# Giving the first eight pairs of a fused attention and gated network due times of their own

## The chip, the core and the metric

The kernel runs on one core of a Trainium2 chip. Its time is the device time of one execution, in microseconds (us); less is better. The engines are TensorE (PE in the profile's rows: matmuls; PEld: its weight loads), VectorE (DVE), ScalarE (ACT), GpSimd (POOL) and SyncE (SP), whose queue issues most transfers (DMA).

## What is computed

Eight batches of eight heads (576 positions, 64 per head, float32) go through rotary attention, and the result of all heads of a batch through a gated network with a causal convolution of 5 taps as its gate.

```python
q_rot, k_rot = rotate(q), rotate(k)            # (8, 8, 576, 64)
scores = scale * np.matmul(q_rot, k_rot.transpose(0, 1, 3, 2))
scores = scores - np.max(scores, axis=-1, keepdims=True)
attn = np.exp(scores)
attn = attn / (np.sum(attn, axis=-1, keepdims=True) + 1e-09)
x = np.matmul(attn, v)                         # heads joined: (8, 576, 512)
...
for k in range(5):
    gate_pre += conv_w[k] * xp[:, k:k + S, :]  # xp: x with 4 zeros in front
gate = 1.0 / (1.0 + np.exp(-gate_pre))
val = x @ w_val
return gate * val @ w_out
```

## The kernel before

The unit of work is a pair of heads, 32 in all, four to a batch. For a pair p the program loads k and q (`loadk`, `loadq`, on SP's queue), rotates them (`mul0`, `mul1`, `add`), splits them into a high and a low part (`hi` on ScalarE, `lo`), and multiplies them on TensorE in five chunks of queries: `s0` to `s3` for the two heads side by side, `s4` for the last 64 queries of both together. Each chunk's rows get a maximum on VectorE (`max0` to `max8`, line 261) and an exponential on ScalarE (`exp0` to `exp8`, line 274); `exp8` writes the tile `pm`. The probabilities are then transposed: in pairs 0 to 4 and in the last one by TensorE (`t0` to `t7`, line 303) with copies out of PSUM (`c0` to `c7`, lines 190 and 192), in the others by VectorE (`x1`, `x3`, `x5`, `x7`, one for each chunk, line 289) with 16 transfers (`mv`). The value products follow (`pv4`, `pv0`, `pv1`, lines 359 to 377), the division by the row sums (`norm`), and the taps of the convolution (`tap0` on ScalarE, `tap1` to `tap4` on VectorE, line 429). `xhi`, `xlo` split the result. After the fourth pair of a batch its network is added (`f00` to `f07` the first product, `f10` to `f17` the second, `od` its evictions, line 463 the matmuls). The weights arrive in pieces and are decoded early, between the first pairs (`lval`, `dval`, `lout`, `dout`); `taps`, `dtap` load and decode the convolution's factors. `warm0` to `warm4` are matmuls without a result that fill TensorE's first stretch.

Nothing of this is written down in the order in which it runs. Each job is given to a planner with a due time and with what it reads and writes; the planner takes the ready job with the earliest due time, again and again, and that order is the order on each engine's queue. So a job stands where the largest due time among itself and the jobs that it waits for puts it. A job that needs a buffer which is not free is parked until one is. The score chunks keep their order through a token (`order`). GpSimd jobs wait for the last VectorE job ahead of them that is marked as using the shared port.

The due time is a base, which grows by `PERIOD` = 18.5 for each pair, plus an offset from the table `DUE`, looked up by the job's name. Pairs 0 to 4 use names with an `e` at the end (`s0e`), pair 0's loads and rotary steps names with `_0` and `_1` for the two parts of the sequence, and all later pairs share one set. The table `PICK` tells for most elementwise steps, copies and transfers which engine does them (V, A, G, SP).

```python
heap = [(jobs[i][0], i) for i in range(len(jobs)) if not left[i]]
...
i = heappop(heap)[1]
...
t = PERIOD * p
...
at(f"s{c}" + ph, t + 3.6 * c, "PE", 830, s_mm, p, c, r=r, w=w + " order", mode="r" if c < 4 else "f")
at(f"max{i}" + ph, t + 3.6 * c + 1 + 0.7 * h, "V", 670, s_max, p, i, r=f"ps_s/{p}.{i}", w=f"nm/{p}.{i}")
at(f"x{i}" + ph, tt, "V", 1270, turn, p, i // 2, cs, r=r + f" p/{p}.{i // 2}#0", w=f"big/T{p}#{i // 2}")
```

Here `tt` is `t + 3.6 * (i // 2) + 3.6 + 0.7 * (i % 2)`. Buffers that matter here: three tiles for scores in PSUM (`ps_s`, one for each head's chunk), two for everything else in PSUM (`ps_t`), three tiles `p` for probabilities.

Of the kernel before, what the change touches and what calls it, by code (L numbers as in the profile page):

```python
# [144 lines left out]
def attn_gated_ffn(ctx: ExitStack, tc: tile.TileContext, q2, k2, v2, tab, w_val, conv_w, w_out, out, collect=None):  # L145
# [4 lines left out]
    V, A, G, T, SP = nc.vector, nc.scalar, nc.gpsimd, nc.tensor, nc.sync  # L150
# [6 lines left out]
    plan = Plan()  # L157
# [353 lines left out]
    taps = []  # L511
# [41 lines left out]
        for t in mixq:  # L553
            V.memset(t.bitcast(F32), 0.0)

    def at(key, base, e, ns, fn, *args, pick=None, r="", w="", kb=0, mode=None, port=False):

        options = ns if pick else None
        if pick:
            e = PICK.get(pick, e)  # L560
            ns, port = options[e]
            args = [ENG[e] if a == "ENGINE" else a for a in args]
        plan.add(base + DUE.get(key, 0.0), e, fn, *args, r=r, w=w, port=port)
        if collect is not None:
            collect.append((key, base, pick, options, ns, kb * (3.6 if fn is move else 2.95), mode, port or e == "G"))

# [34 lines left out]
    PERIOD = 18.5  # L601
    for p in range(NP):
        t = PERIOD * p
        par = p % 2
        last = p == NP - 1
        ph = "e" if p < EARLY else ""
        cs = TURNED.get(p, (0, 1, 2, 3) if p >= EARLY and not last else ())
        xt = toks(f"x{par}#@", range(5))
        for n in ("k", "q"):
            cut = 288 if n == "k" else 256  # L610
# [105 lines left out]
        last = b == NB - 1  # L716
# [92 lines left out]
```

## Time and profile before

| what | value |
|---|---|
| median of 3 runs | 649.25 us (648.69 to 650.76) |
| the profiled execution | 645.8 us, of it 644.0 us from the first to the last instruction (the span) |
| TensorE busy | 612.9 us (95%) |
| VectorE busy | 569.8 us (88%) |
| ScalarE busy | 463.7 us (72%) |
| GpSimd busy | 404.6 us (63%) |
| moved by DMA | 134.43 MB |
| granted TensorE clock, mean | 0.997 of full speed |

Times in the rows below are counted from the start of the span. Busy shares are means over stages that differ: an early one in which weights are decoded and probabilities are transposed on TensorE, a long steady one, and an end without new pairs. An engine that is idle costs nothing unless the last engine to finish waits for it.

### The profile page before, as it was taken

To read this page: it belongs to the slowest core of one execution; us is meant where nothing else is said; L and a number is where in the kernel's file an instruction comes from. 1 tells how busy PE (TensorE), PEld (TensorE's weight loads), DVE (VectorE), ACT (ScalarE), POOL (GpSimd) and SP (SyncE) were. 2 spreads that over 40 slices of the span, in tenths; PEclk is the share of its full clock that TensorE was granted. 3 is DMA by queue.
4 is the path that set the end of the run, shared out by engine and by line. 5 is a ranking of instruction groups with operands and counts; after the bars stand their busy time and mean duration, and the time that the engine had idled before them with its cause. 6 is when DMAs were issued, how large, how long until landed. Compare 5 with 4: busy or idle time off the path is not lost.

```text
span 644.0 us, 15384 instructions
## 1 busy us (share of the span) xinstructions
PE 612.9 (95%) x5683; PEld 502.1 (78%) x5683; DVE 569.8 (88%) x820; ACT 463.7 (72%) x1161; POOL 404.6 (63%) x304
## 2 busy tenths in 40 slices
PE   8899998989999999999999999999899999999897
PEld 8666665778787887888788887887688878888797
DVE  5998899988999999999999999999999999995452
ACT  4989988767777777777777768776777778765421
POOL 4433457776778868796868868785878768730300
PEclk9999999989999999999999999999999999999999
DMA  6524532379999999989999899898999998864011
GB/s 234 196 69 167 178 114 75 111 202 251 267 259 241 260 263 258 276 236 259 242 261 258 236 266 251 251 251 233 245 267 257 249 274 249 214 168 127 29 49 54
DMA packets 51482, 134.43 MB, mean 209 GB/s; under 512 B 10928, under 2 KB 20944, under 8 KB 51408
## 3 DMA queue, kind: packets, MB, share of 16 engines
q1 hardware_dynamic: 50864, 132.86, 73.1%
q8 instruction: 45, 0.74, 0.5%
q10 hardware_dynamic: 544, 0.59, 0.3%
q14 instruction: 29, 0.24, 0.1%
HBM read 62.48 MB, written 9.59 MB: 112 GB/s over the span
## 4 chain that ended last, share of the span: by engine, by line
PE 73%; DVE 13%; DMA 4%; ACT 4%; POOL 2%; issue 2%; SPq 1%; DVEq 0%; POOLq 0%; ACTq 0%
PE ps_t L463 29%; PE ps_s L255 17%; PE ps_t L369 17%; DVE nm L261 5%; PE ps_t L359 3%; DVE g L429 3%; DVE big L289 2%; PE ps_t L374 2%; PE ps_t L330 2%; ACT p L274 2%; DMA big<-big 2%; PE ps_t L303 1%; POOL xl L416 1%; DMA rb<-rd 1%; PE ps_t L345 1%
## 5 line engine op out<-in xcount | busy, mean ns | idle before, releaser
L261 DVE TENSOR_REDUCE nm<-ps_s 128x1 f32<-128x576 f32 x288 | 203.3, 743 | 18.2 <-PE ps_s L255 18.1
L274 ACT ACTIVATE p<-ps_s,nm 128x576 f32<-128x576 f32 x256 | 187.6, 738 | 34.1 <-DVE nm L261 31.2
L255 PE MATMUL ps_s<-k,q 64*128 64x288 f32 x1536 | 144.1, 311 | 11.7 <-ACT p L274 9.6
L289 DVE STREAM_TRANSPOSE big<-p 128x1152 f32<-128x1152 f32 x104 | 140.6, 1360 | 0.0
L255 PEld LDWEIGHTS ps_s<-k,q 64*128 64x128 f32 x1536 | 110.5, 185 | 36.1 <-issue 15.5
L429 DVE SCALAR_TENSOR_TENSOR g<-x,cw,g 128x576 f32<-128x576 f32 (+1 forms) x132 | 117.3, 890 | 1.8 <-ACT g L426 1.5
L369 PE MATMUL ps_t<-big,v 128*64 128x256 f32 (+2 forms) x1024 | 118.4, 382 | 0.0
L212 POOL TENSOR_TENSOR iq<-iq,tab 128x576 f32<-128x576 f32 (+2 forms) x60 | 84.6, 1428 | 35.7 <-DMA iq<-in_q 25.7
L369 PEld LDWEIGHTS ps_t<-big,v 128*64 128x64 f32 x1024 | 70.1, 137 | 44.6 <-issue 13.9
L463 PE MATMUL ps_t<-xh,wval_hi 128*128 128x288 f32 x256 | 79.7, 311 | 0.4 <-DVE x L405 0.3
L463 PE MATMUL ps_t<-yh,wout_hi 128*128 128x288 f32 x256 | 79.4, 311 | 0.0
L216 POOL TENSOR_TENSOR ik<-ik 128x576 f32<-128x576 f32 (+1 forms) x28 | 50.5, 1804 | 45.9 <-DVE ik L212 44.0
L463 PE MATMUL ps_t<-yl,wout_hi 128*128 128x288 f32 x256 | 76.3, 298 | 1.8 <-POOL yl L476 1.8
L463 PE MATMUL ps_t<-xl,wval_hi 128*128 128x288 f32 x256 | 76.5, 299 | 0.5 <-POOL xl L416 0.5
L463 PE MATMUL ps_t<-xh,wval_lo 128*128 128x288 f32 x256 | 76.0, 297 | 0.0
L463 PE MATMUL ps_t<-yh,wout_lo 128*128 128x288 f32 x256 | 76.0, 297 | 0.0
L476 POOL TENSOR_TENSOR yl<-g,yh 128x288 fp32r<-128x288 f32 x56 | 46.8, 835 | 46.4 <-ACT yh L472 42.6
L227 POOL TENSOR_TENSOR k<-ik,k 128x576 fp32r<-128x576 f32 x31 | 49.7, 1603 | 35.3 <-ACT k L223 35.1
L416 POOL TENSOR_TENSOR xl<-x,xh 128x576 fp32r<-128x576 f32 x31 | 47.7, 1538 | 20.2 <-ACT xh L412 18.3
L463 PEld LDWEIGHTS ps_t<-xh,wval_hi 128*128 128x128 f32 x256 | 49.1, 192 | 4.3 <-issue 2.3
L274 ACT ACTIVATION_READ_ACCUMULATOR p<-ps_s,nm 128x1 f32 x256 | 50.7, 198 | 0.0
L463 PEld LDWEIGHTS ps_t<-yh,wout_hi 128*128 128x128 f32 x256 | 48.9, 191 | 2.2 <-PE ps_s L255 1.8
(95 smaller groups left out, 1081.8 us busy)
## 6 DMA issues: line engine op xcount, KB each, us to landing
big<-big SPq DMA_DIRECT2D x416, 144.0 KB
ik<-in_k SPq DMA_DIRECT2D x31, 576.0 KB
iq<-in_q SPq DMA_DIRECT2D x31, 576.0 KB
v<-in_v SPq DMA_DIRECT2D x32, 320.0 KB
rb<-rd SPq DMA_DIRECT2D x64, 144.0 KB
out_t<-oo SPq DMA_DIRECT2D x64, 144.0 KB
big<-in_w_val SPq DMA_DIRECT2D x4, 512.0 KB
big<-in_w_out SPq DMA_DIRECT2D x4, 512.0 KB
```

What stands on the lines that cost most here:

```text
L212: eng.tensor_tensor(out=t[:, i, a:b], in0=t[:, i, a:b], in1=tabs[:, i, a:b], op=ALU.mult)
L216: eng.tensor_tensor(out=t[:, 0], in0=t[:, 0], in1=t[:, 1], op=ALU.add)
L227: eng.tensor_tensor(out=t[:, 1], in0=state[p][n + "in"][:, 0, a:b], in1=t[:, 0].bitcast(F32), op=ALU.subtract)
L255: T.matmul(out=ps[:, half, 0:288], lhsT=st["q"][rows, x, c * 128:c * 128 + 128] if c < 4 else mixq[p % 2][:, x], rhs=st["k"][rows, y, k0:k ...
L261: V.tensor_reduce(out=st[f"nm{i}"], in_=st[f"s{i}"], axis=AX.XY, op=ALU.max, negate=True)
L274: A.activation(out=pd.rearrange("p (b x) -> p b x", b=2), in_=st[f"s{i}"], func=AF.Exp, bias=st[f"nm{i}"], scale=1.0, accum_out=sums[p % 2 ...
L289: V.transpose(out=t[:, :, cs.index(c)].rearrange("p b k i -> p k b i"), in_=st[f"p{c}"].rearrange("p h s -> p (h s)").rearrange("p (k b i) ...
L369: T.matmul(out=acc[HEAD[h], 0:n], lhsT=st["v"][:, j, h, :], rhs=st["pt"][:, :, c0:c1, 5 * place(p, 2 * c0 + h) + j].rearrange("p a c i -> ...
L416: eng.tensor_tensor(out=st["xl"][:, a:b], in0=xs[p % 2][:, 4 + a:4 + b], in1=st["xh"][:, a:b].bitcast(F32), op=ALU.subtract)
L429: V.scalar_tensor_tensor(out=g, in0=x_sb[:, a + k:b + k], scalar=w, in1=g, op0=ALU.mult, op1=ALU.add)
L463: T.matmul(out=acc[:, 0:n], lhsT=wt[w][:, kc, ds], rhs=mv, start=(kc == 0 and i == 0), stop=(kc == NCH - 1 and i == 2))
L476: eng.tensor_tensor(out=ffn[b, "l", dc, lo], in0=y, in1=ffn[b, "h", dc, lo].bitcast(F32), op=ALU.subtract)
```

## The change

Three lines of code change: the lookups of `DUE` and `PICK` try the name with `@` and the pair's number first, for pairs 0 to 7 (`OWN` = 8). A batch's network is added inside its fourth pair's turn, so batches 0 and 1 use the numbers 3 and 7. `DUE` grows from 267 to 811 entries; the old ones without a number keep their values where pairs from 8 on use them. `PICK` grows from 98 to 270; 36 of its new entries name another engine than the old table, and no old one changes. `TURNED` is empty, so the line with it gives the same as before. The tables are cut below to entries that the text speaks of, one to a line.

```diff
+OWN = 8
...
-DUE = {
...
-'dtap': 18.1213, 'max0e': 14.6821, 'max1e': 13.2885, 'tap2e': 19.0603, 'tap3e': 21.309,
-'pv4e': 18.8053, 'loadke': -59.771, 'loadqe': -41.1482, 'lval0': -12.7532,
-'s0': 9.932, 's3': 21.9753, 's4': 23.5471, 'max0': 16.779, 'max1': 14.6677, 'max8': -12.7968,
-'exp6': -0.0862, 'x5': 22.804, 'x7': 22.26,
...
+DUE = {
...
+'dtap': -69.8201, 'max0e@0': -61.4337, 'max1e@0': -56.4516, 's0e@0': -10.8488, 'tap2e@4': 34.8082, 'tap3e@4': 43.1084,
+'pv4e@0': 19.0091, 'pv4e@1': 18.2196, 'pv4e@2': 18.1959, 'pv4e@3': 21.281, 'pv4e@4': 19.3977,
+'loadke@1': 25.2513, 'loadqe@1': 20.8687, 'lval0': -21.5969,
+'s3@5': 15.9488, 's4@5': -6.7157, 'max8@5': -8.7262, 'exp6@5': 20.7505, 'x5@5': 21.4718, 'x7@5': -16.7783,
+'s0@6': -11.4168, 'max0@6': -39.7509, 'max1@6': -3.4868,
...
+PICK: from G to V
+  'kadd_1@0', 'qmul1_0@0', 'qlo_0@0', 'qadd_1@0' (parts of the sequence),
+  'xloe@0', 'qmul1e@1', 'kmul1e@4', 'klo@5', 'qmul0@5', 'qadd@5', 'qmul0@6', 'qmul1@6', 'kmul0@7', 'klo@7'
+PICK: from V to G
+  'qmul0e@2', 'kmul1@5', 'kmul1@6', 'kmul1@7'
+PICK: from A to V
+  'c1e@0', 'c1e@1', 'c2e@1', 'cme@1', 'c6e@2', 'c3e@3', 'cme@3', 'cm@6',
+  'ch1e@3', 'qmixede@4', 'chm@7', 'od1@7', 'od2@7'
+PICK: from V to A
+  'c4e@1', 'c0e@2', 'c4e@2', 'c4e@3', 'c0e@4'
...
+    phase = [0]
+
     def at(key, base, e, ns, fn, *args, pick=None, r="", w="", kb=0, mode=None, port=False):
...
-            e = PICK.get(pick, e)
+            e = PICK.get(f"{pick}@{phase[0]}", PICK.get(pick, e))
...
-        plan.add(base + DUE.get(key, 0.0), e, fn, *args, r=r, w=w, port=port)
+        plan.add(base + DUE.get(f"{key}@{phase[0]}", DUE.get(key, 0.0)), e, fn, *args, r=r, w=w, port=port)
...
         t = PERIOD * p
+        phase[0] = p if p < OWN else ""
...
-        cs = TURNED.get(p, (0, 1, 2, 3) if p >= EARLY and not last else ())
+        cs = TURNED.get(-1 if last else p, (0, 1, 2, 3) if p >= EARLY and not last else ())
```

## Rows read from the trace of the kernel before

**Rows 1.** Busy us by stage: PE, PEld, DVE, ACT, POOL; then clock, DMA, GB/s.

```profile
0.00:20.00 20.00, 16.52 (x129) 14.98 (x130) 13.08 (x26) 9.76 (x21) 8.36 (x14) 1.00 0.72 255
20.00:120.00 100.00, 91.06 (x795) 63.49 (x793) 94.00 (x146) 87.33 (x209) 48.86 (x33) 1.00 0.35 118
120.00:180.00 60.00, 56.16 (x497) 47.65 (x498) 54.06 (x75) 43.42 (x113) 44.42 (x35) 0.97 0.84 229
180.00:560.00 380.00, 370.70 (x3593) 306.32 (x3592) 360.45 (x496) 286.37 (x730) 290.92 (x214) 1.00 0.92 253
```

**Rows 2.** The chain that ended last: start, length, what.

```profile
217.74 3.60 PE ps_t L369 x32
...
410.30 3.60 PE ps_t L369 x32
```

**Rows 3.** TensorE's waits from 20 to 180 us: total, times, longest.

```profile
PE ps_s L255 <- ACT p L274: 4.7, 8, 1.1
PE ps_t L303 <- ACT big L190: 2.1, 3, 1.1
PE ps_s L255 <- ACT pm L274: 2.0, 1, 2.0
```

**Rows 4.** Timeline of TensorE near 130 us (start, length, what, idle before).

```profile
129.40 1.06 PE L255 MATMUL ps_s<-k,q 64*128 64x288 f32 x12
132.43 0.40 PE L255 MATMUL ps_s<-k,q 64*128 64x288 f32 x1 [1.97 <-ACT pm L274]
133.39 1.05 PE L255 MATMUL ps_s<-k,q 64*128 64x288 f32 x11 [0.56 <-ACT p L274]
```

**Rows 5.** Timeline of VectorE in the same stretch.

```profile
129.51 1.36 DVE L289 STREAM_TRANSPOSE big<-p 128x1152 f32<-128x1152 f32 x1
130.80 2.04 DVE L261 TENSOR_REDUCE nm<-ps_s 128x1 f32<-128x576 f32 x3
```

**Rows 6.** Busy time by stretches of 2 us behind it; PEclk follows POOL.

```profile
134.00:136.00 2.00, 2.00 (x15) 1.84 (x12) 2.00 (x4) 2.00 (x5) 1.26 (x1) 0.69 0.97 226
136.00:138.00 2.00, 2.00 (x11) 1.72 (x11) 1.74 (x2) 1.17 (x6) 2.00 (x3) 0.50 0.97 228
```

**Rows 7.** VectorE's groups from 0 to 200 us (busy us, mean ns, idle before).

```profile
L261 DVE TENSOR_REDUCE nm<-ps_s 128x1 f32<-128x576 f32 x92 | 65.6, 744 | 5.4 <-PE ps_s L255 5.3
L429 DVE SCALAR_TENSOR_TENSOR g<-x,cw,g 128x576 f32<-128x576 f32 x30 | 30.8, 1026 | 0.0
...
L212 DVE TENSOR_TENSOR ik<-ik,tab 128x576 f32<-128x576 f32 x10 | 7.5, 751 | 0.0
L192 DVE COPY big<-ps_t 128x512 f32<-128x512 f32 x10 | 6.8, 683 | 1.4 <-PE ps_t L303 1.4
...
L216 DVE TENSOR_TENSOR iq<-iq 128x576 f32<-128x576 f32 x4 | 4.2, 1052 | 0.4
...
L216 DVE TENSOR_TENSOR ik<-ik 128x576 f32<-128x576 f32 x4 | 3.0, 758 | 0.4
...
L212 DVE TENSOR_TENSOR iq<-iq,tab 128x256 f32<-128x256 f32 x1 | 0.4, 426 | 0.8 <-DMA iq<-in_q 0.8
```

**Rows 8.** Timeline of VectorE: two taps.

```profile
113.45 1.97 DVE L429 SCALAR_TENSOR_TENSOR g<-x,cw,g 128x576 f32<-128x576 f32 x1
...
128.45 0.77 DVE L429 SCALAR_TENSOR_TENSOR g<-x,cw,g 128x576 f32<-128x576 f32 x1
```

**Rows 9.** Timeline of GpSimd beside the first of them.

```profile
112.86 1.94 POOL L216 TENSOR_TENSOR iq<-iq 128x576 f32<-128x576 f32 x1 [0.48 <-DVE big L503]
```

**Rows 10.** GpSimd's largest group from 0 to 200 us.

```profile
L212 POOL TENSOR_TENSOR iq<-iq,tab 128x576 f32<-128x576 f32 x18 | 26.4, 1481 | 10.0 <-DMA iq<-in_q 4.6 <-DVE big L499 2.9 <-DVE g L429 2.0
```

**Rows 11.** Timeline of GpSimd in pair 0's rotary steps.

```profile
6.54 0.96 POOL L212 TENSOR_TENSOR iq<-iq,tab 128x256 f32<-128x256 f32 x1 [5.24 <-DMA iq<-in_q]
```

**Rows 12.** Timeline of VectorE: the addition behind it, and a tap-decoding step.

```profile
7.54 1.00 DVE L216 TENSOR_TENSOR iq<-iq 128x256 f32<-128x256 f32 x1 [0.62 <-POOL iq L212]
...
31.96 0.18 DVE L502 SCALAR_TENSOR_TENSOR oo<-oo,oo 128x20 f32<-128x20 f32 x1
```

More of the change, by code (lines that the diff above doesn't have):

```diff
@@ L36 @@
-PICK = {'c0': 'V', 'c0e': 'V', 'c1': 'A', 'c1e': 'A', 'c2': 'V', 'c2e': 'A', 'c3': 'V', 'c3e': 'A', 'c4': 'A', 'c4e': 'V', 'c5': 'V', 'c5e': 'A', 'c6': 'V', 'c6e': 'A', 'c7': 'A', 'c7e': 'A', 'ch0': 'A', 'ch0e': 'V', 'ch1': 'A', 'ch1e': 'A', 'chm': 'A', 'chme': 'A', 'cm': 'A', 'cme': 'A', 'kadd': 'G', 'kadd_0': 'V', 'kadd_1': 'G', 'kadde': 'V', 'kfront': 'A', 'kfronte': 'A', 'klo': 'G', 'klo_0': 'V', 'klo_1': 'V', 'kloe': 'G', 'kmul0': 'G', 'kmul0_0': 'V', 'kmul0_1': 'V', 'kmul0e': 'V', 'kmul1': 'V', 'kmul1_0': 'V', 'kmul1_1': 'V', 'kmul1e': 'G', 'od0': 'A', 'od0l': 'V', 'od1': 'A', 'od1l': 'V', 'od2': 'A', 'od2l': 'A', 'od3': 'A', 'od3l': 'A', 'qadd': 'G', 'qadd_0': 'V', 'qadd_1': 'G', 'qadde': 'V', 'qlo': 'G', 'qlo_0': 'G', 'qlo_1': 'G', 'qloe': 'G', 'qmixed': 'A', 'qmixede': 'A', 'qmul0': 'G', 'qmul0_0': 'V', 'qmul0_1': 'V', 'qmul0e': 'V', 'qmul1': 'G', 'qmul1_0': 'G', 'qmul1_1': 'G', 'qmul1e': 'G', 'xlo': 'G', 'xloe': 'G', 'xlol0': 'V', 'xlol1': 'V', 'ylo': 'G', 'ylol': 'V', 'ch3': 'V', 'ch3e': 'A', 'decout': 'A', 'decval': 'A', 'odma': 'SP', 'odmal': 'SP', 'loadk': 'SP', 'loadk_0': 'SP', 'loadk_1': 'SP', 'loadke': 'SP', 'loadq': 'SP', 'loadq_0': 'SP', 'loadq_1': 'SP', 'loadqe': 'SP', 'loadv': 'SP', 'loadve': 'SP', 'mv0': 'SP', 'mv1': 'SP', 'mv2': 'SP', 'mv3': 'SP', 'rr': 'SP', 'rre': 'SP', 'rw': 'SP', 'rwe': 'SP'}
```

3 lines of the change are left out of this document (2 added, 1 removed).

## The prediction

> **What bounds the kernel now.** I read the busy windows by stage first [rows 1]. TensorE is busy for 370.7 of the 380 us from 180 to 560, so the long middle, which the change leaves as it is, runs at TensorE's pace: the value products that open pairs 9 and 20 begin at 217.74 and 410.30, eleven pairs apart, which is 17.5 us a pair [rows 2]. Time can be won only where TensorE stands still or runs slowly before that. Its idle time is 3.5 us of the first 20, 8.9 us of 20 to 120 and 3.8 us of 120 to 180, 16.2 us in all, and this is the ceiling for the part of the program that the change orders anew. A microsecond won there should reach the end, because from then on TensorE has a backlog.
>
> Next, why it stands still. From 20 to 120 us VectorE is busy for 94.0 us and ScalarE for 87.3 us, GpSimd for 48.9 us [rows 1]: three engines share the early pace, and VectorE has the least room. TensorE's waits in 20 to 180 us [rows 3] name ScalarE's exponentials (4.7 and 2.0 us) and its copies out of PSUM (2.1 us). An exponential waits for its maximum, which is VectorE's, so one asks what VectorE was doing. The largest single place shows it [rows 4, 5]: TensorE ends the first scores of pair 6 at 130.46 (129.40 + 1.06), waits 1.97 us for the exponential of pair 5's last tile (pm), and 0.56 us for one more. In that time VectorE works through a transposition of 1.36 us (128x1152), and only then takes the three maxima that were asked for. And the pause is paid twice: in the next stretches the granted clock is 0.69 and 0.50 of full speed [rows 6], that is, it fell to the lower level (1.2 GHz) after the pause. Two stretches of 2 us at 0.69 and 0.50 lose 0.6 + 1.0 = 1.6 us against full clock.
>
> Last, what makes VectorE late. The taps (scalar_tensor_tensor, 128x576) average 1026 ns over the first 200 us [rows 7], while an undisturbed one takes 0.77 us and one beside a GpSimd instruction 1.97 us [rows 8, 9]. Thirty taps at 0.256 us too much are 7.7 us; the rotary addition of q (1052 ns against 758 ns for that of k, four times) adds 1.2 us. I count about 9 us of such stretching in 0 to 200 us.
>
> The Trainium skill, page "SBUF — State Buffer", section "Who interferes with whom", states that a VectorE instruction with two SBUF inputs and a GpSimd instruction that reads SBUF exclude each other for a whole instruction, and that a reduction is exempt. The trace agrees: 0.77 against 1.97 us for the tap, and a steady 744 ns for the maximum. By that rule the change cuts both ways: the work brought to VectorE from GpSimd has two SBUF inputs and can be blocked itself; with every one of those 14 blocked for one GpSimd instruction of about 1.4 us the sum would lose some 20 us, with none blocked it would lose nothing.
>
> **The change, part by part.** *Code executed.* The same matmuls, reductions, exponentials and transfers run; no byte is added. What changes is the place of an instruction on its engine's queue for pairs 0 to 7 (and of batches 0 and 1's network), and 36 choices of engine.
>
> *Engine choices.* From GpSimd to VectorE go 4 partial and 10 whole elementwise steps: 4 x 0.43 + 10 x 0.75 = 9.2 us more for VectorE [rows 7]. Back go 4 whole ones: -3.0 us. From ScalarE to VectorE go eight PSUM copies of 512 columns (0.683 us each), and one of 256 columns, two casts of pair 4, one copy of 128, and four output evictions of 288 (0.25 to 0.43 us each, my estimate from the 256-column row of [rows 7], halved for the smallest): 5.5 + 2.9 = 8.4 us. Five 512-column copies go to ScalarE: -3.4 us. VectorE gets 9.2 - 3.0 + 8.4 - 3.4 = 11.2 us more; 5.5 us of it are in pairs 0 to 4 (1.7 us of these, the partial steps, before 20 us). GpSimd loses, net, six whole steps (1.48 us each [rows 10]) and four partial ones (0.96 us [rows 11]); ScalarE loses, net, three large copies and eight smaller pieces. VectorE has 6.0 us idle in 20 to 120 us and 5.9 us in 120 to 180 [rows 1], so this lies beside other work only if a good part of the 9 us of stretching goes with the GpSimd steps that leave. Bounds: +0 if it all goes, and the 11.2 us against 11.9 us idle if none does. I take half of the stretching gone, which leaves VectorE about 7 us heavier and almost without slack, and I charge 2.0 us for new waits of TensorE.
>
> *The order around pairs 5 and 6.* A job's place is the largest due time among itself and those that it waits for. Base plus offset gives for pair 5: scores s3 125.3 before (5 x 18.5 + 3 x 3.6 + 21.98) and 119.2 after, s4 130.4 and 100.2 (so 119.2, behind s3), the transposition x5 126.8 and 125.5, x7 129.9 before and after 125.9 (its own 90.8 is overruled by exp6, 125.9). The first scores of pair 6 are held by s4 through the order token: 130.4 before, about 119 after; their maxima 130.4 before and about 119 to 121 after. So before, x5 and x7 stand ahead of max8 of pair 5 and max0 and max1 of pair 6, which is the stall of [rows 4, 5]; after, these three maxima stand ahead of both. The network of batch 0, which is to fill TensorE, keeps its place (125 to 130 in both). I take this stall as gone: 1.97 + 0.56 + 1.6 of clock = 4.1 us. Bounds: 0, if the wait only moves to the next transposition, and 4.1.
>
> *The rest of the order in pairs 0 to 4.* TensorE's 8.9 us idle in 20 to 120 us come in waits of 0.2 to 1.1 us. Some causes move: the first pair's max0 and max1 go from due 16 and 15 to -11 (right behind their scores), ahead of the weight decoding that stood between them; several PSUM copies that TensorE waited for change to the other engine. Others stay (max3 of pair 0 still comes behind pair 1's rotary steps). I take a quarter, 2.2 us; bounds 0 and 8.9.
>
> *The start.* The transfers of pair 0 keep their order. Three partial rotary steps leave GpSimd, which shortens the chain to the first scores: GpSimd's 0.96 us multiplication [rows 11] and the addition that waits 0.62 us for it [rows 12]. Against this the seven tap-decoding steps come from the span around 29 to 34 us to the head of VectorE's queue, some 1.2 us at 0.18 us each [rows 12] with a wait for their small transfer, and ScalarE's cast of k now stands behind that of q. I take 0.3 us later; bounds -0.6 and +1.0.
>
> *Moved and put at nothing.* Pair 1's loads stand behind the first weight load on SP's queue now, hidden by pair 0's own rotary steps and scores, which come first on every engine; without that cover they are later by one 512 KB load, 2.0 us at the 255 GB/s of the first 20 us [rows 1]. Taps 2 and 3 of pair 4 go later (123.6 to 139.3 and 127.3 to 149.1), hidden until batch 1's network wants the gate; it is 1.6 us of VectorE work pushed from a full stretch into one with 5.9 us idle.
>
> **Sum.** -4.1 (pairs 5 and 6) - 2.2 (pairs 0 to 4) + 0.3 (start) + 2.0 (VectorE's new load) = -4.0 us. Against the profiled execution's own 645.8 us (span 644.0 and 1.8 around it) that is 641.8. The median of the runs shown is 649.25, 3.4 us above that execution; the same difference gives 645.2 us.
>
> **The rivals.** *The gain is larger.* With six whole and four partial GpSimd steps fewer the collisions of VectorE go as well; then its new load costs nothing and about half of the 8.9 us comes back: -4.1 - 4.5 + 0.3 = -8.3, 641. For it: the taps alone carry 7.7 us of excess. Against it: most GpSimd steps stay.
>
> *Given back.* The stall at 130 us is mended but VectorE, 11.2 us heavier, delays other maxima by as much; or the order differs only where nothing waited, as the value products keep their due times (40, 58, 77, 95, 114 before; 40, 58, 76, 98, 114 after). 649 us, within 0.3%.
>
> *Slower.* VectorE becomes the bound in 20 to 120 us. It needs 94.0 + 3.8 = 97.8 of 100 us there if the taps still collide, and each of the three whole steps brought there from GpSimd that meets a GpSimd step adds up to 1.2 us (1.97 - 0.77). From two such meetings on it needs more than the stretch has, and each microsecond goes to TensorE by way of the maxima, with one more fall of the clock at 1.6 us: +4 us, 653. For it: 94% busy already, and GpSimd half idle there gives work away. Against it: the steps that leave GpSimd are ones to collide with. The exclusion that the page on SBUF states is this rival's mechanism; no row of before shows it for a step that is moved.
>
> **How the numbers follow.** A difference under 0.3% (1.9 us) is what a measurement of this kernel can't tell from none. Chances: the forecast 0.45 (643 to 647 us), the larger gain 0.15, given back 0.22, slower 0.18. Faster 0.60, same 0.22, slower 0.18. The range reaches from the larger gain to most of the slower case: 641 to 651; I leave about 0.08 below and 0.10 above.
>
> **What would show it.** In the profile after, value products that open pair 9 (L369) should begin about 4 us before 217.74, and the span should end by as much earlier. The wait of scores on pm near 130 us and the clock of 0.5 behind it should be missing. Mean time of the taps in the first 200 us should fall from 1026 toward 900 ns; if it stays and VectorE is above 97% busy in 20 to 120 us, the slower case is at work. If pair 9 comes 4 us earlier and the end does not, the backlog argument was wrong.

## The result and the profile after

The kernel became slower: 652.62 us median (650.42 to 657.84, 13 runs) against 648.62 (645.19 to 651.46, 13 runs), ratio 1.0069 [1.0045, 1.0094]. With the runs made later beside the experiments the medians are 652.5 (25 runs) and 648.6 (99). The profiled execution took 653.56 us, span 651.8, at a mean clock of 0.992. Its line numbers are one higher than those of before (the scores are L256, the maxima L262).

Busy time by stage of after, columns as in [rows 1]:

```profile
0.00:20.00 20.00, 15.97 (x127) 14.29 (x127) 14.40 (x36) 9.36 (x20) 3.94 (x9) 1.00 0.73 258
20.00:120.00 100.00, 88.27 (x740) 62.95 (x740) 92.08 (x143) 79.78 (x192) 36.86 (x24) 0.97 0.35 118
120.00:180.00 60.00, 57.07 (x526) 46.70 (x522) 58.14 (x81) 44.45 (x114) 44.73 (x35) 1.00 0.76 209
180.00:560.00 380.00, 369.23 (x3546) 305.80 (x3546) 363.20 (x493) 282.99 (x723) 288.15 (x213) 1.00 0.91 251
```

TensorE does less from 20 to 120 us (88.3 us against 91.1) and more from 120 to 180. VectorE (third of the busy times) is no busier from 20 to 120 us than before, 92.1 against 94.0 us, and GpSimd falls from 48.9 to 36.9. TensorE's waits from 20 to 180 us, beside [rows 3]:

```profile
PE ps_t L346 <- DVE pm L387: 4.9, 4, 1.5
PE ps_t L304 <- ACT wval_lo L191: 1.7, 1, 1.7
PE ps_t L304 <- ACT p L275: 1.4, 4, 0.5
...
PE ps_s L256 <- ACT p L275: 0.5, 2, 0.3
```

The scores' waits for the exponentials and for pm are nearly gone (0.5 us); a new wait, of a transposition, is the largest, four times for VectorE's reciprocal of the row sums (L387), near 54, 76, 116 and 137 us. Where [rows 4 to 6] had the stall, TensorE is now busy without a break, up to the last of these waits (1.49 us, from 135.6 on), and its clock is full (start and end, length, TensorE busy, clock, DMA share, GB/s):

```profile
130.00:132.00 2.00, 2.00 (x17) 1.00 0.13 23
132.00:134.00 2.00, 2.00 (x17) 1.00 0.80 277
134.00:136.00 2.00, 1.60 (x17) 1.00 0.33 73
```

But behind two of the new waits the clock halves, and 3.4 us of full speed are lost, each stretch of 2 us times what its clock lacks:

```profile
54.00:56.00 2.00, 1.22 (x8) 0.86 0.00 0
56.00:58.00 2.00, 1.99 (x9) 0.50 0.01 2
58.00:60.00 2.00, 2.00 (x22) 0.79 0.79 174
74.00:76.00 2.00, 0.97 (x12) 0.98 0.28 113
76.00:78.00 2.00, 2.00 (x10) 0.50 0.01 2
78.00:80.00 2.00, 2.00 (x17) 0.67 0.26 74
```

VectorE and GpSimd ahead of the first of them:

```profile
51.28 1.40 DVE L498 TENSOR_SCALAR big<-big 128x512 int32<-128x512 int32 x1
52.71 1.79 DVE L500 SCALAR_TENSOR_TENSOR big<-big 128x512 int32<-128x512 int32 x1
54.43 0.20 DVE L387 RECIPROCAL pm<-sums 128x9 f32<-128x9 f32 x1
```

```profile
50.99 1.41 POOL L213 TENSOR_TENSOR iq<-iq,tab 128x576 f32<-128x576 f32 x1 [3.98 <-DMA iq<-in_q]
52.42 1.53 POOL L213 TENSOR_TENSOR ik<-ik,tab 128x576 f32<-128x576 f32 x1
```

Two weight-decode steps stand ahead of the reciprocal, each stretched beside a GpSimd multiplication (1.40 and 1.79 us; the same two take 0.41 and 0.68 at 68.8 and 70.3). The sums had been ready since 49.49 (49.28 + 0.21).

The begin of each pair's value products tells where the time goes. After minus before: pair 0 +1.67 us, pair 1 +3.43, pair 2 +5.82, pair 3 +6.40, pair 4 +7.39 (119.17 against 111.78), pair 5 +2.87, pair 9 +3.63, pair 31 +7.34 (before begins it at 605.19). So 7.4 us are lost up to pair 4, 4.5 come back between pairs 4 and 5, where the stall was, and 4.5 more are lost behind pair 5, 3.7 of them behind pair 9, where nothing is changed.

### The profile page after: what moved, and what is told of

It is laid out like the page before. It is cut to its first block, busy times and chain, and to the rows that moved or that the text cites. A ratio compares the mean times of both kernels' runs of the same rounds, so it can differ in the third digit from the quotient of the medians.

```text
span 651.8 us, 15381 instructions
## 1 busy us (share of the span) xinstructions
PE 615.8 (94%) x5683; PEld 504.6 (77%) x5683; DVE 583.1 (89%) x841; ACT 458.7 (70%) x1150; POOL 393.0 (60%) x294
## 4 chain that ended last, share of the span: by engine, by line
PE 50%; DVE 21%; DMA 9%; POOL 8%; issue 5%; ACT 3%; SPq 2%; POOLq 0%; DVEq 0%; ACTq 0%
PE ps_t L464 20%; PE ps_s L256 12%; PE ps_t L370 10%; DVE nm L262 6%; DMA big<-big 5%; DVE big L290 5%; DVE g L430 4%; DMA iq<-in_q 2%; SPq L295 2%; POOL iq L213 2%; PE ps_t L360 2%; PE ps_t L304 2%; PE ps_t L331 1%; PE ps_t L375 1%; POOL yl L477 1%
## 5 line engine op out<-in xcount | busy, mean ns | idle before, releaser
L262 DVE TENSOR_REDUCE nm<-ps_s 128x1 f32<-128x576 f32 x288 | 202.8, 742 | 17.5 <-PE ps_s L256 17.1
L256 PE MATMUL ps_s<-k,q 64*128 64x288 f32 x1536 | 142.4, 311 | 7.9 <-ACT p L275 6.7
L256 PEld LDWEIGHTS ps_s<-k,q 64*128 64x128 f32 x1536 | 110.1, 186 | 30.9 <-issue 14.8
L213 POOL TENSOR_TENSOR iq<-iq,tab 128x576 f32<-128x576 f32 (+1 forms) x56 | 79.1, 1431 | 49.5 <-DMA iq<-in_q 29.3
L217 POOL TENSOR_TENSOR ik<-ik 128x576 f32<-128x576 f32 x27 | 49.4, 1830 | 41.3 <-DVE ik L213 38.4
L228 POOL TENSOR_TENSOR k<-ik,k 128x576 fp32r<-128x576 f32 x29 | 45.8, 1579 | 31.4 <-ACT k L224 28.0
L213 POOL TENSOR_TENSOR ik<-ik,tab 128x576 f32<-128x576 f32 x32 | 46.8, 1462 | 14.7 <-DVE iq L213 5.8
L228 POOL TENSOR_TENSOR q<-iq,q 128x576 fp32r<-128x576 f32 (+1 forms) x32 | 45.3, 1415 | 16.7 <-ACT q L224 16.7
```

Source lines behind the costliest of these rows:

```text
L213: eng.tensor_tensor(out=t[:, i, a:b], in0=t[:, i, a:b], in1=tabs[:, i, a:b], op=ALU.mult)
L217: eng.tensor_tensor(out=t[:, 0], in0=t[:, 0], in1=t[:, 1], op=ALU.add)
L228: eng.tensor_tensor(out=t[:, 1], in0=state[p][n + "in"][:, 0, a:b], in1=t[:, 0].bitcast(F32), op=ALU.subtract)
L256: T.matmul(out=ps[:, half, 0:288], lhsT=st["q"][rows, x, c * 128:c * 128 + 128] if c < 4 else mixq[p % 2][:, x], rhs=st["k"][rows, y, k0:k ...
L262: V.tensor_reduce(out=st[f"nm{i}"], in_=st[f"s{i}"], axis=AX.XY, op=ALU.max, negate=True)
```

## The experiments

"p0" is the begin of pair 0's value products, "p0-4" the time from there to pair 4's, "p4-5" to pair 5's, "VectorE" its busy time in p0-4, all from each kernel's profiled execution; us and ratio are the median and its ratio to before, timed beside it.

| kernel | us | ratio | p0 | p0-4 | VectorE | p4-5 |
|---|---|---|---|---|---|---|
| before | 648.62 | 1 | 34.73 | 77.05 | 71.95 | 35.24 |
| before again (e12) | 648.6, one run | | 35.99 | 77.15 | 72.02 | 35.25 |
| after | 652.62 | 1.0069 | 36.40 | 82.77 | 75.48 | 30.72 |
| after again (e11) | 651.53 | 1.0055 [1.0022, 1.0088] | 37.39 | 80.86 | 75.21 | 30.74 |
| e1 new due times, old engines | 664.61 | 1.0261 [1.0221, 1.0301] | 39.66 | 89.18 | 73.81 | 35.61 |
| e2 old due times, new engines | 668.56 | 1.0327 [1.0291, 1.0362] | 37.38 | 89.82 | 71.53 | 37.90 |
| e3 pairs 5 to 7 alone | 668.93 | 1.0321 [1.0282, 1.0360] | 34.88 | 86.53 | 73.95 | 40.52 |
| e4 pairs 0 to 4 alone | 666.89 | 1.0309 [1.0274, 1.0344] | 38.20 | 89.27 | 76.66 | 39.42 |
| e5 after, multiplications late | 660.78 | 1.0169 [1.0118, 1.0220] | 36.83 | 93.75 | 75.70 | 31.98 |
| e6 after, thm late | 658.51 | 1.0155 [1.0102, 1.0207] | 36.29 | 84.96 | 76.06 | 33.03 |
| e7 before, s4 of pair 5 early | 651.98 | 1.0037 [1.0006, 1.0068] | 38.52 | 76.75 | 70.94 | 37.82 |
| e8 after, e5 and e6 | 659.72 | 1.0175 [1.0130, 1.0220] | 35.89 | 91.16 | 75.10 | 33.33 |
| e9 after, reciprocals early | 650.66 | 1.0022 [0.9992, 1.0051] | 40.20 | 80.75 | 75.14 | 32.02 |
| e10 after, TensorE kept busy | 651.01 | 1.0028 [0.9999, 1.0057] | 38.06 | 80.95 | 75.39 | 32.07 |
| e13 after, less for VectorE | 648.92 | 0.9997 [0.9962, 1.0032] | 37.54 | 78.63 | 71.03 | 32.02 |
| e15 after, more for VectorE | 655.50 | 1.0113 [1.0068, 1.0159] | 40.89 | 87.64 | 77.44 | 30.84 |
| e14 before, less for VectorE | 654.35 | 1.0104 [1.0067, 1.0141] | 38.47 | 76.42 | 67.31 | 39.62 |
| e16 before, more for VectorE | 656.49 | 1.0119 [1.0068, 1.0169] | 38.30 | 79.89 | 74.57 | 36.14 |
| e17 after, five copies to ScalarE | 654.12 | 1.0100 [1.0070, 1.0131] | 37.17 | 84.20 | 72.01 | 30.72 |
| e18 after, three copies, reciprocals early | 654.98 | 1.0087 [1.0052, 1.0122] | 36.22 | 81.18 | 73.08 | 32.00 |

### Which part loses: due times or engines, early or late pairs

At the start two theories stood against each other: A, the new order's place for `thm` (the row sums' transposition, L346) makes TensorE wait; B, VectorE's added load does, the slower rival. Four kernels take the change apart: e1 has every new due time and the old engine choices, e2 the reverse (the order does not depend on the choices), e3 the entries of pairs 5 to 7 alone, e4 those of pairs 0 to 4, the weights and batch 0's network.

```diff
 e1: DUE of after, PICK of before        e2: DUE of before, PICK of after
 e3: before + entries @5, @6, @7          e4: before + entries @0 to @4, dtap, weights, network of batch 0
```

> All new due times, but every engine choice as before the change. Theory A (the order: TensorE's transposition thm of pairs 0 to 4 stands right behind a reciprocal that VectorE reaches late, and the clock falls after the wait): the waits of L346 for the reciprocal stay at 3 us or more in all, pair 4's value products begin at least 5 us later than before the change, pair 5 gives back about 4 us as in the changed kernel, and the time is 650 to 653 us. Theory B (VectorE's 11.2 us of added work): with that work gone the early pairs keep their old pace, the gain at pair 5 remains, and the time is 644 to 646 us.

> All old due times, with the 36 new engine choices. Theory A (order): no wait for the reciprocal, pair 4's value products within 2 us of before the change, 648 to 651 us. Theory B (load): VectorE busy above 97% from 20 to 120 us, pair 4 at least 4 us later than before the change, 652 to 655 us.

> New due times and engine choices for pairs 5 to 7 and batch 1's network alone; pairs 0 to 4 and the weights as before. Both theories put the loss in pairs 0 to 4: pair 4 within 0.5 us of before the change, the wait near 130 us gone, pair 5 to 7 about 3 to 4 us earlier than before, 644 to 646 us. If the time stays at 648.6 us, the gain of 4.5 us between pair 4 and pair 5 in the changed kernel was only the return of work that its own delay had pushed together, and the mended stall was worth nothing.

> New due times and engine choices for pairs 0 to 4, the weights and batch 0's network alone; pairs 5 to 7 as before. Both theories: pair 4's value products about 7 us later than before, as in the changed kernel. If the stall near 130 us is a matter of pairs 5 and 6's own due times, it stays and the time is 655 to 657 us; if it only fills a hole that a late pair 4 leaves no room for, the time is as of the changed kernel, 652 to 653 us.

Measured: each part alone costs 17 to 22 us, the whole 4. Every expected time missed, and no additive account can hold: new engines with the old order +21, the old engines with the new order +17, both +4. e3 shows how a part fails: with pairs 5 to 7 alone moved, pair 4's value products already come 9.5 us later, and long single waits stand before and behind them (start, length, idle before):

```profile
116.81 0.33 PE L346 MATMUL ps_t<-ident,pm 128*128 128x128 f32 x1 [2.94 <-ACT big L191]
129.18 1.81 PE L256 MATMUL ps_s<-k,q 64*128 64x288 f32 x11 [2.30 <-ACT p L275]
143.59 1.07 PE L256 MATMUL ps_s<-k,qm 128*128 128x288 f32 x6 [2.37 <-ACT qm L191]
```

An order and its engine choices fit each other or they don't. A part of this table is a third kernel, not a share of the second, so the later runs leave the order as it is wherever they can.

### The places named by the traces

e5 puts the early multiplications, which stretch the decode steps, back to their old due times in pairs 2 to 4 (five of the six are GpSimd's in after, that of k in pair 4 is VectorE's); e6 puts `thm` of pairs 1, 2, 4 and 5 one or two jobs later on TensorE; e8 does both; e7 is before with only the scores that released the stall of [rows 4, 5] moved.

```diff
 e5: 'qmul1e@2..4': 12.2307, 'kmul1e@2..4': 11.8756
 e6: 'thme@1': 16.9, 'thme@2': 17.8, 'thme@4': 20.1, 'thm@5': 18.7
 e7: before + 's4@5': 15.0
```

> The changed kernel with six due times as before: GpSimd's second rotary multiplications (mul1) of k and q in pairs 2 to 4, which the change lets start as soon as their load lands. Theory C (place of the collision: these multiplications stretch weight-decoding steps that stand on VectorE's queue right ahead of the reciprocal and a maximum that TensorE waits for, and the clock falls behind each wait): the weight steps at 51 to 54 us and at 73 us fall to 0.4 to 0.7 us, the waits of L346 at 54.8 and 76.0 us (1.38 and 1.02 us) go, and with them the half clock behind both (3.4 us); 647 to 649 us. Theory A (it is TensorE's own order that puts thm too early): the waits stay or move, 651 to 653 us.

> The changed kernel with the transposition thm of pairs 1, 2, 4 and 5 one to two jobs later on TensorE's queue, so that other work covers the wait for the reciprocal. Theory A: the waits of L346 for the reciprocal (4.9 us in all) and the half clock behind two of them (3.4 us) go, 646 to 648 us. Theory C: VectorE is late anyway, and the next instruction that needs it waits in the place of thm (scores waiting for an exponential, or a transposition for its copy); less than half comes back, 650 to 653 us.

> The kernel before with one due time changed: the last scores of pair 5 (s4) behind s3 at once, which brings max8 of pair 5 and max0 and max1 of pair 6 ahead of the transposition x7 on VectorE's queue. If the stall near 130 us was worth what the prediction gave it, 1.97 and 0.56 us of waiting and 1.6 us of half clock go and the time is 643 to 645 us. If the wait only moves to the next late maximum, or TensorE lacks the network's matmuls there afterwards, 647 to 650 us.

> The changed kernel with both the six old due times of mul1 and the later thm. If the two stand for one loss (a wait and its cause), this is no better than the better one of them, within 1 us. If they add, it is 2 us or more below each.

Measured: e5, e6 and e8 are 6 to 8 us slower than after's 652.6; e5 and e6 lie above both of their expected ranges. In e5 the later multiplication makes a VectorE addition wait 4.4 us, and through an exponential TensorE once waits for 5.73 us. In e7 the wait for pm and the half clock near 130 us are gone, yet pair 4 to 5 takes 37.8 us and not 35.2, and the median is 2.3 us above that of before, beyond both expected ranges: the maxima come earlier, the transpositions later, and TensorE waits at 138.80 for the network's gate product and for the next exponentials:

```profile
138.80 0.40 PE L464 MATMUL ps_t<-xh,wval_hi 128*128 128x288 f32 x1 [1.33 <-DVE g L469]
...
141.86 1.05 PE L256 MATMUL ps_s<-k,q 64*128 64x288 f32 x11 [0.88 <-ACT p L275]
```

So the move in which I had seen the end of the stall takes the wait away and doesn't shorten the stretch, which now holds 3.2 us more of VectorE's work (35.70 us against 32.52 in before again). That the stretch is short in after (30.7 us) rests on more of its order.

### Are the waits the cause, or a sign?

e9 moves three instructions of 0.20 us, the reciprocals of pairs 1, 2 and 4, ahead of the decode steps, and nothing else on any engine. e10 leaves the order and gives TensorE eight transpositions of the identity to do where it waited. e11 and e12 are after and before once more.

```diff
 e9:  'rinve@1', '@2', '@4': ahead of dval3, dout1, dout0   ('thme' keeps its place)
 e10: in hm_mm, for p in (1, 2, 4, 5):
+        for _ in range(8):
+            T.transpose(out=state[p]["bhm"][:, 0:128], in_=ident, identity=ident)
```

> The kernel after with three instructions moved on VectorE's queue and nothing else: the reciprocals of pairs 1, 2 and 4 (0.20 us each) go ahead of the weights' decode steps behind which they stood; their sums had been ready 4.9, 3.5 and 1.6 us before they ran. Theory A (the lost 7.4 us of pairs 0 to 4 are in good part the three waits of TensorE for these reciprocals, 1.38 + 1.02 + 1.00 us, and the 3.4 us that the halved clock costs behind two of them): the waits go, the clock stays full at 54 to 60 and 74 to 80 us, pair 4's value products begin 3 us and not 7.4 us behind before's, and the time is 647 to 649.5 us. Theory D (the whole order and the engine choices hang together, and what comes earlier is lost at the next wait): the waits at these places go, others come, and the time is 651 to 658 us.

> The kernel after with eight transpositions of the identity added on TensorE ahead of the row sums' transposition of pairs 1, 2, 4 and 5, into the same bank, so that TensorE is busy while it would wait for the reciprocal; the order is untouched. Theory of the clock (the halved clock behind two of these waits costs 3.4 us that the end sees): the clock stays full at 54 to 60 and 74 to 80 us, and the time is 649 to 650.5 us, pair 4's value products 4 to 5 us behind before's. Theory D (what TensorE does earlier it waits for at the next tile): the clock stays full, but pair 4 begins 7 us late as before and the time is 652 to 654 us.

> The kernel after, unchanged, beside the two others: 651 to 654 us, and its waits for the reciprocal near 54, 76 and 117 us come again within 1 us of their size if they belong to the order; if they come from how the loads of one execution happened to land, other places show them.

> The kernel before, unchanged, for a second trace: 644 to 652 us; the wait for pm near 130 us and the half clock behind it come again if they belong to the order, and pair 0's value products begin at 34.7 us if the 3.8 us by which the kernel before with s4 of pair 5 moved began them late came from a load that landed 1.1 us late.

Measured: the waits go in e9 and the clock is full at 54 to 60 and 74 to 80 us in both, but p0-4 is 80.75 and 80.95 us, as in after again (80.86). In e9 TensorE waits at the next transposition (`tm`) instead:

```profile
PE ps_t L331 <- ACT pq L191: 2.5, 2, 1.4
```

Theory A falls: taking those waits away gains nothing; they are where TensorE stands while something else sets the pace. e10 even gives TensorE 2.9 us more to do in these pairs (74.00 against 71.10), and they take no longer. The medians, 0.9 and 0.5 us below after again, are within the intervals, and lie between the two expected ranges. After again has the same waits (1.42 and 1.02 us) with the clock full behind them, and its p0-4 is 1.9 us shorter than in the first trace: the halved clock is the only difference in these pairs that I found.

The two repeats have an undisturbed clock up to pair 4, so they are the pair to compare. Pair by pair, from p0 to pair 4 and in a last row from pair 4 to pair 5: length, then TensorE, its loads, VectorE, ScalarE, GpSimd; then clock, DMA, GB/s. Before again:

```profile
35.99:56.98 20.99, 18.89 (x164) 13.18 (x164) 19.54 (x30) 17.87 (x44) 7.34 (x5) 1.00 0.42 137
56.98:75.57 18.59, 17.65 (x161) 12.62 (x160) 16.96 (x29) 17.13 (x41) 7.81 (x5) 1.00 0.46 155
75.57:94.94 19.37, 17.97 (x160) 12.65 (x159) 18.00 (x25) 17.02 (x42) 11.11 (x8) 1.00 0.37 126
94.94:113.14 18.20, 15.43 (x136) 10.48 (x136) 17.52 (x26) 15.19 (x37) 11.78 (x8) 1.00 0.23 82
113.14:148.39 35.25, 32.53 (x266) 26.30 (x266) 32.52 (x45) 25.78 (x65) 27.73 (x22) 0.95 0.57 160
```

After again:

```profile
37.39:59.15 21.76, 19.36 (x164) 13.32 (x163) 19.99 (x30) 16.84 (x42) 7.50 (x5) 1.00 0.30 103
59.15:79.22 20.07, 17.93 (x162) 12.78 (x160) 19.25 (x29) 16.95 (x41) 6.13 (x4) 1.00 0.49 170
79.22:99.06 19.84, 17.77 (x161) 12.63 (x160) 18.00 (x32) 16.63 (x40) 7.60 (x5) 1.00 0.29 97
99.06:118.25 19.19, 16.04 (x149) 11.48 (x148) 17.97 (x29) 15.49 (x36) 8.32 (x7) 1.00 0.35 119
118.25:148.99 30.74, 29.23 (x256) 24.15 (x254) 29.46 (x41) 24.55 (x63) 26.42 (x21) 1.00 0.61 173
```

In both kernels VectorE is idle for only 0.7 to 1.8 us in each pair up to pair 4. After gives it 3.2 us more to do in these four pairs (75.21 - 72.02), and they take 3.7 us longer (80.86 - 77.15). The busy share of a fixed stretch hides this: when pairs take longer, less of the work falls into the stretch.

But a milestone tells when one job begins, not that the same work lies ahead of it. In after again a chunk of twelve score matmuls stands right ahead of pair 4's value products:

```profile
117.27 1.05 PE L256 MATMUL ps_s<-k,q 64*128 64x288 f32 x12
```

In before again it comes behind them (193 records of the line of scores up to there and 108 from there to pair 5; in after again 205 and 98). And what VectorE has more to do up to pair 4, 3.2 us, it has less to do from there to pair 5, 3.1 us (29.46 against 32.52). From p0 to pair 5 the work is level again, 883 matmul records each and 104.7 against 104.5 us of VectorE's work. Over this whole stretch after again is not slower but 0.8 us faster (111.60 us against 112.40), although 1.7 us of that is the half clock of before again near 136 us, which it does not have.

The chain that ended last, by line over these pairs, has VectorE's maxima and taps at 18.1 and 9.4% in after again, and TensorE's value products at 8.9%; in before again the value products lead, 18.8%, and maxima and taps have 16.4 and 11.3%.

### VectorE's work as the only thing changed

In these four the order and the engines stay; the second of the six decode steps of each weight chunk (0.68 us each, eight chunks) is left out, so that the weights lack sign and top exponent bit, or done twice.

```diff
     def weight_step(n, c, k):
+        if k != 1:                            # e13, e14
+        for _ in range(2 if k == 1 else 1):   # e15, e16
             wsteps[n, c][0][k]()
```

> The kernel after without the second of the six decode steps of each of the eight weight chunks (0.68 us each undisturbed, 8 of them, 5.4 us of VectorE's work between 20 and 120 us; the output then lacks the sign and the top bit of the weights' exponents), the order and the engine choices untouched. Theory B (VectorE's work sets the pace of pairs 0 to 4, 1 us of work for 0.9 us of time): pair 4's value products begin 4 to 5.5 us earlier than in after, only 1 to 3 us behind before's, and the time is 647 to 649.5 us. Theory D (the loss lies in the order's waits, and VectorE's idle 6% would hide a few us): pair 4 moves by less than 1.5 us and the time stays at 651 to 653 us.

> The same step left out of the kernel before. Theory B: VectorE sets the pace of pairs 0 to 4 here too, pair 4 begins 4 to 5 us earlier (near 108 us); the wait near 130 us swallows a part, so the time is 644 to 647 us. Theory D: pair 4 within 1.5 us of before, 648 to 650 us.

> The kernel after with that decode step done twice (the second run changes nothing in the result; 5.4 us more for VectorE, somewhat more where GpSimd runs beside). Theory B: pair 4 begins 4.5 to 6 us later than in after, 11 to 13 us behind before, and the time is 655.5 to 658.5 us. Theory D: under 2 us, 651 to 654 us.

> The kernel before with that decode step done twice. Theory B: pair 4 begins 4.5 to 6 us later, that is about as late as in after, without the stall at 130 us mended, so the time is 652 to 655 us. Theory D: 648 to 651 us.

Measured from p0 to pair 4, as time for work: after, -4.2 us of work give -2.2 us, and +2.2 give +6.8 (the clock is at 0.84 and 0.89 in two of those pairs); before, -4.7 give -0.7, and +2.6 give +2.7. That looks like a bend, from one trace each: in before a further microsecond of VectorE's work costs one and a saved one brings almost nothing; after stands beyond it. Theory B has the sign and, in after, the medians (-2.6 and +4.0 from 651.5), at less than the full size. It fails for e14: p0-4 shrinks by only 0.7 us and the whole is 5.7 us slower. In its trace TensorE waits once, near 125 us, for the last weight chunk, behind a ScalarE cast that waits for GpSimd:

```profile
125.17 0.79 PE L540 MATMUL ps_t<-wout_hi,minus 128*128 128x512 f32 x1 [3.79 <-ACT wout_hi L535]
```

```profile
123.92 0.67 ACT L223 CAST q<-iq 128x576 fp32r<-128x576 f32 x1 [5.67 <-POOL iq L216]
```

### Handing work back

```diff
 e17: PICK 'c2e@1', 'cme@1', 'c6e@2', 'c3e@3', 'cme@3': 'V' -> 'A'
 e18: PICK 'c2e@1', 'c6e@2', 'c3e@3': 'V' -> 'A', and the due times of e9
```

> The kernel after with five of its copies out of PSUM in pairs 1 to 3 back on ScalarE, where before had them (c2 and cm of pair 1, c6 of pair 2, c3 and cm of pair 3: 0.68 us each on VectorE, 3.4 us in all; 0.60 each on ScalarE), the order untouched. Theory B (VectorE's work sets the pace of pairs 0 to 4): pair 4's value products begin 1.5 to 3 us earlier than in after, and the time is 648.5 to 650.5 us. Theory D (choices and order were fitted to each other, and ScalarE's exponentials would come later): 653 to 660 us.

> The kernel after with only the three of these copies that no wait of TensorE's mixed rows hangs on (c2 of pair 1, c6 of pair 2, c3 of pair 3) back on ScalarE, 2.0 us off VectorE, and the reciprocals of pairs 1, 2 and 4 ahead of the decode steps as in e9. Theory B: 648 to 650 us, level with before or just ahead of it, and ahead of e9's 650.7. Theory D: 652 to 658 us.

Measured: neither gains; VectorE's 75.2 us become 72.0 and 73.1, p0-4 is 84.2 (the clock at 0.92 and 0.93 in two pairs, as in after's first trace) and 81.2 us. In e17 the chain's maxima and taps fall to 4.1 and 2.8%, and ScalarE's exponentials and copies have 11.2 and 8.1% (3.3 and 2.6% in after again): ScalarE's chain lies right behind VectorE's. Both medians lie where theory D, choices and order fitted to each other, had put them. And e18, with its clock full, bears on the cause: VectorE has 73.1 us to do and ScalarE 67.2 (before again: 72.0 and 67.2), and the four pairs still take 81.2 us and not 77.2. Loads near before's don't bring before's time back in after's order. No version beat before.

## Why the prediction was wrong

The forecast was -4.0 us, measured +4.0. The step that failed is VectorE's new load together with the gain in pairs 0 to 4: +2.0 and -2.2 by the prediction, +3.7 us measured from p0 to pair 4 with the clock full, +5.7 with it halved. With pairs 5 and 6 (-4.1) the prediction had -4.3 us from p0 to pair 5; the repeats show -0.8, the first traces +1.2 (113.49 against 112.29). Pair 9 was to come 4 us earlier; it comes 0.7 us later between the repeats (218.91 against 218.21) and 3.6 later between the first traces.

- **Pairs 5 and 6, -4.1.** The size came near, -4.5 us between pairs 4 and 5 (30.72 against 35.24), in part by luck. Between the repeats 1.7 us of it are the clock, which is full, and 1.2 TensorE's idle time (2.72 against 1.51 us): some 2.9 us for what the prediction priced at 4.1, because a wait of 1.5 us moved to the next transposition, the case that it had named for its lower bound. The other 1.6 us are work that after does ahead of pair 4. The reason was too narrow as well: e7 makes the named move alone and gains nothing.
- **VectorE's load, +2.0.** Mis-sized in its price, not in its amount. Up to pair 9 VectorE has 7.1 us more to do between the repeats (204.3 against 197.2), the "about 7 us" of the prediction; 3.8 of them come ahead of p0 and 3.2 ahead of pair 4. The prediction set 5.5 us more in pairs 0 to 4 against idle time of 6.0 us and against stretching that would leave. The stretching of the taps did fall, from 1026 ns to 907 over the first 200 us, but the idle time was none to be used: each of the four pairs keeps 0.7 to 1.8 us of it, in either kernel. How much of the 3.7 us is VectorE's work stays open. e16 gives 1.07 us of time for each added microsecond in before's order; after's 3.2 us by that rate are 3.4 us. e13 gets 2.2 us back for 4.2 of work; by that rate they are 1.7. e18 moves 2.1 us of work to ScalarE and gets nothing back. So VectorE's work moves the pace, but its part and the order's were not separated, and about 1 us is the score chunk that now stands ahead of pair 4.
- **Pairs 0 to 4, -2.2.** Not there. Waits of TensorE went and others took their places, and e9 and e10 show that such waits can be removed without gaining anything.
- **The start, +0.3.** It is +1.67 between the first traces and +1.40 between the repeats, past the upper bound of 1.0. VectorE's work ahead of p0 grew by 2.8 and 3.8 us; that this is the reason was not tested.
- **The backlog.** By pair 5 after again is 0.6 us behind before again (1.97 against 1.37 behind the first trace of before), after 2.9 behind before. The medians differ by 4. From pair 5 to pair 31 single executions of one program drift apart by several us (after +4.5, after again -1.6, before again +1.5, all against before's first), so two traces of each don't tell what part of the last 1 to 3 us the change causes. Nor do the other kernels whose order from pair 5 on is the same: eight traces with after's order (after, after again, e9, e10, e13, e15, e17, e18) take 456.6 to 464.5 us there, 460.9 in the mean, and four with before's (before, before again, e14, e16) 457.8 to 461.0, in the mean 459.2. The granted clock is not the reason: its means over all runs are 0.990 for after and 0.991 for before, and a straight line of time against clock, with one slope for both kernels, leaves after 3.4 us slower at the same clock. So the loss in the medians is measured, its place behind pair 5 is not found, and this stays open.
- **The slower rival.** Sign and size were its (+4 us, 653), and its mechanism is borne out in part: VectorE's load moves the pace of pairs 0 to 4, but between the repeats only 0.6 us of the loss are there at pair 5. Its signs in the profile did not show: VectorE is not above 97% busy from 20 to 120 us (92.1% in after, 94.3% in after again), and the taps' mean did fall. The page "SBUF — State Buffer" of the Trainium skill, section "Who interferes with whom", counts tensor_scalar, the first decode step, among the operations that can contend with GpSimd for their shared port, and says that a VectorE instruction with two SBUF inputs, as the second has, contends with a GpSimd instruction that reads SBUF; the rows at 51 us agree (0.41 to 1.40, 0.68 to 1.79 us). e9 shows that the reciprocal's place behind these two steps is not what decided.

## What to carry to other kernels

Ask of a wait whether it sets the pace: move what is late by one place, or give the waiting engine something to do, and see whether the next milestone comes earlier. Compare engines' busy time between milestones of the work, not in a fixed stretch, and see that the same work lies between them: a new order moves work across a milestone too. Don't count on idle time that comes in each unit of work. When the work of three engines in a unit lies as close together as here (within 0.7 to 3.2 us a pair), a saving on one is worth what the next chain leaves of it, and half of a fitted order with its engine choices can be worse than none (here 17 to 22 us against 4).

## What the runs showed of the hardware that was not expected

- The granted clock fell to half behind TensorE's waits of 1.38 and 1.02 us in one execution of after and stayed full behind the same waits, 1.42 and 1.02 us, in another.
- In the trace of e7, whose order at the start is before's, a rotary table that landed later let VectorE's first q step begin at 7.59 us and not at 6.50. Pair 0's value products came 3.8 us later, with the clock at half near 12 and 22 us. In before again the same step began at 7.76 us, the clock stayed full (1.00 up to p0), and they came 1.3 us later. So the late landing alone does not make the 3.8 us.
